# The copy of the low value tile on GpSimd, behind the masks and the weighting, from chunk 2 on

## The chip, the core and the metric

The kernel runs on one core of a Trainium2 chip. The metric is the time of one execution in microseconds (us) on the device. The core has five engines with queues of their own, each executed in order: TensorE (PE in the profile, PEld for its weight loads), VectorE (DVE), ScalarE (ACT), GpSimd (POOL) and SyncE (SP). They wait for each other through semaphores.

## The reference

Two layers follow each other. The first is causal attention with a forget gate, over 8 batches, 8 heads, 576 positions and 64 values a head; the second is a dense layer with a GELU between two products, over 4608 tokens.

```python
# q, k, v: (8, 8, 576, 64), f: (8, 8, 576)
scores = scale * np.matmul(q, k.transpose(0, 1, 3, 2))
cum = np.cumsum(np.log(np.clip(f, 0.0001, 1.0)), axis=-1)
scores = np.where(causal, -1000000000.0, scores + cum[:, :, :, None] - cum[:, :, None, :])
attn = softmax(scores)                                  # with its maximum subtracted
x = matmul(attn, v).transpose(0, 2, 1, 3).reshape(4608, 512)
h = x @ w_in                                            # w_in: (512, 2048)
out = gelu_tanh(h) @ w_out                              # w_out: (2048, 512)
```

## The kernel before

**Attention.** The 64 pairs of batch and head are worked as 16 quads of four heads, quad i from 0 to 15. The decay is folded into the values: `make_vw` multiplies the values of a quad by a weight for each key (line 214) and writes the bf16 tile `vw[i % 2]`, of which there are two. The mul is made by GpSimd where the order says `VW` and by VectorE where it says `vw`. The tile has five slots for the 576 keys in blocks of 128, and a sixth, `LOW`. From quad 2 on, the first 64 queries with the first 64 keys are a piece of their own, whose keys lie on partitions 64 to 127; `copy_low` (line 219) therefore copies the values of those 64 keys from slot 0, partitions 0 to 63, into slot `LOW`, partitions 64 to 127. That is 64 partitions by 256 bf16 values. It can be made once `make_vw` of the same quad is done, and the product that reads it is the next one of that quad.

The other steps of a quad are, by their words in the order: `TK` and `TQ`, transposes of keys and queries by VectorE (line 197); `S`, a third of the scores on TensorE (line 260), with the exponential by ScalarE (line 268); `M`, causal masks by GpSimd with affine selects (line 274), or `m`, the same by a product on VectorE (line 303); `D`, the denominators: a product with the weights themselves (tile `w_bf`, line 328), then transpose, reciprocal and transpose on VectorE (lines 347 to 351); `V`, the two halves of attention times values (tiles `vw` and `po`, line 328), each followed by a VectorE mul into `xT` (line 359). The accumulator `po` has one buffer, so the second `V` waits until VectorE has read the first.

**Dense layers.** The tokens are worked in nine chunks c of 512. The products of chunk c are cut into seven instead of eight (sums of blocks made beforehand), with `P` and `R` for the first layer (lines 373 and 432) and `F`, `f` and `O` for so many matmuls of the second (line 527). VectorE adds the partial products of the second layer from PSUM (line 552, tiles `o_st` and `snap`); TensorE's next product into the same bank waits for that. `T` are the sums of blocks for the next chunk (line 405). `LK`, `LQ` load keys and queries through GpSimd's DMA queue (line 191).

**Order.** The order is written out by hand, as words in `FRONT` and, for chunks 2 to 8, in `TABLES`; every engine's queue holds its instructions in that order. `q3` in the table of chunk c stands for quad 2c + 3, so chunk 2 starts on quads 7 (`q3`) and 8 (`q4`). `CL` is the copy of the low tile. Before the change the words about it in chunks 3 to 5 are

```
VW.q3 f.18 S.q3.2 V.q2.1 M.q3.2 TK.q5 CL.q3 f.16 S.q4.0 VW.q4 D.q3
M.q4.0 f.18 S.q4.1 TQ.q5 V.q3.0 M.q4.1 f.13 V.q3.1 T f.3 CL.q4 S.q4.2
```

Chunk 2 has the same words there. Chunk 6 has only quad 15 left, so one `CL`. On VectorE `CL.q3` thus stands behind the transposes of keys `TK.q5` and ahead of an add of line 552, `D.q3`, a second add, `TQ.q5` and the mul of `V.q3.0`. On GpSimd `VW.q3` stands ahead of the masks `M.q3.2`, which stand ahead of `VW.q4`.

Of the kernel before, what the change touches and what calls it, by code (L numbers as in the profile page):

```python
# [16 lines left out]
def kernel(  # L17
# [10 lines left out]
    nc = tc.nc  # L28

    B, H, S, D = q.shape  # L30
# [36 lines left out]
    LOW, HIGH = NT, NT - 1  # L67
# [18 lines left out]
    TABLES = {}  # L86
    TABLES[2] = """
        Y O.512 P.0.1 R.1 P.4.1 R.1 R.1 TK.q3 TQ.q3 LK.q5 LQ.q5 m.q2.1 M.q2.2.2 m.q2.0 m.q2.2.3 CL.q2 LV P.2 G.0 P.3 K.3.0 K.3.1 K.3.2 P.6 P.7 K.3.3
        G.1.1.2 X F.10 S.q3.0 D.q2 M.q3.0 f.22 S.q3.1 V.q2.0 TK.q4 TQ.q4 M.q3.1 VW.q3 f.18 S.q3.2 V.q2.1 M.q3.2 TK.q5 CL.q3 f.16 S.q4.0 VW.q4 D.q3
        M.q4.0 f.18 S.q4.1 TQ.q5 V.q3.0 M.q4.1 f.13 V.q3.1 T f.3 CL.q4 S.q4.2  # L90
    """
    TABLES[3] = """
        Y O.512 LK.q4 LQ.q4 P.0.1 R.1 P.4.1 R.1 R.1 LK.q5 LQ.q5 M.q2.2 LV R.3 P.2.1 R.3 G.0.1.2 P.6 R.3 G.0.3.4 G.1.1.2 X F.10 S.q3.0 D.q2 M.q3.0
        f.22 S.q3.1 V.q2.0 TK.q4 TQ.q4 M.q3.1 VW.q3 f.18 S.q3.2 V.q2.1 M.q3.2 TK.q5 CL.q3 f.16 S.q4.0 VW.q4 D.q3 M.q4.0 f.18 S.q4.1 TQ.q5 V.q3.0
        M.q4.1 f.13 V.q3.1 T f.3 CL.q4 S.q4.2
    """
    TABLES[4] = """
        Y O.512 LK.q4 LQ.q4 P.0.1 R.1 P.4.1 R.1 R.1 LK.q5 LQ.q5 M.q2.2 LV R.3 P.2.1 R.3 G.0.1.2 P.6 R.3 G.0.3.4 G.1.1.2 X F.10 S.q3.0 D.q2 M.q3.0
        f.22 S.q3.1 V.q2.0 TK.q4 TQ.q4 M.q3.1 VW.q3 f.18 S.q3.2 V.q2.1 M.q3.2 TK.q5 CL.q3 f.16 S.q4.0 VW.q4 D.q3 M.q4.0 f.18 S.q4.1 TQ.q5 V.q3.0
        M.q4.1 f.13 V.q3.1 T f.3 CL.q4 S.q4.2  # L100
    """
    TABLES[5] = """
        Y O.512 LK.q4 LQ.q4 P.0.1 R.1 P.4.1 R.1 R.1 LK.q5 LQ.q5 M.q2.2 LV R.3 P.2.1 R.3 G.0.1.2 P.6 R.3 G.0.3.4 G.1.1.2 X F.10 S.q3.0 D.q2 M.q3.0
        f.22 S.q3.1 V.q2.0 TK.q4 TQ.q4 M.q3.1 VW.q3 f.18 S.q3.2 V.q2.1 M.q3.2 TK.q5 CL.q3 f.16 S.q4.0 VW.q4 D.q3 M.q4.0 f.18 S.q4.1 TQ.q5 V.q3.0
        M.q4.1 f.13 V.q3.1 T f.3 CL.q4 S.q4.2
    """
    TABLES[6] = """
        Y O.512 P.0.1 R.1 P.4.1 R.1 R.1 LK.q5 LQ.q5 M.q2.2 LV R.3 P.2.1 R.3 G.0.1.2 P.6 R.3 G.0.3.4 K.0.0 K.0.1 K.0.2 G.1.1.2 X F.10 S.q3.0 D.q2
        M.q3.0 f.22 S.q3.1 V.q2.0 M.q3.1 VW.q3 f.18 S.q3.2 V.q2.1 M.q3.2 CL.q3 f.20 D.q3 f.18 V.q3.0 v.q3.1 T f.14 K.0.3
    """  # L110
    TABLES[7] = """
        Y O.512 R.1.1 R.1 p.2 R.1 R.1 R.0.1 R.1 R.0 p.2 R.0 R.0 R.3.1 R.0 R.3 p.6 R.3 R.3 p.6 R.3 G.0.1.2 G.1.1.2 G.0.3.4 F.40 T
# [14 lines left out]
    def many(n, shape, dtype, name):  # L127
        return [singles.tile(shape, dtype, name=f"{name}{i}") for i in range(n)]
# [10 lines left out]
    vw = many(2, [128, NT + 1, 4, D], BF16, "vw")  # L139
# [5 lines left out]
    u1, u2, u4 = many(3, [128, HF, HD], BF16, "usum")  # L145
# [18 lines left out]
    def load_v(b, h0=0, nh=H, ts=range(NT), eng=nc.sync):  # L164
        ins = []
        for t in ts:
            n = min(128, S - 128 * t)
            ins.append(eng.dma_start(  # L168
                out=v_nat[b % 2][:n, t, h0:h0 + nh, :],
                in_=v[b, h0:h0 + nh, 128 * t:128 * t + n, :].rearrange("h p d -> p h d"),  # L170
            ))
        return ins
# [37 lines left out]
    def make_vw(i, eng, part=None):  # L210
        h0 = 4 * (i % QPB)
        vb = v_nat[(i // QPB) % 2]
        t0, t1 = {None: (0, NT), 0: (0, QA // 128), 1: (QA // 128, NT)}[part]
        eng.tensor_mul(  # L214
            vw[i % 2][:, t0:t1], vb[:, t0:t1, h0:h0 + 4, :],
            wT[:, i, t0:t1, :].unsqueeze(3).to_broadcast([128, t1 - t0, 4, D]))

    def copy_low(i):
        nc.vector.tensor_copy(vw[i % 2][64:128, LOW], vw[i % 2][0:64, 0])

    def key_columns(i, key, h, c):

# [172 lines left out]
    def x_blocks(c):  # L395

        new, old = xT[:, :, CH * c:CH * (c + 1)], xT[:, :, CH * (c - 1):CH * c]
        return [z[:, 2 * a:2 * a + 2, HC * b:HC * (b + 1)] for z in (new, old) for a in range(2) for b in range(2)]
# [8 lines left out]
    def w_blocks(k):  # L407

        n = 256
        a11, a12, a21, a22 = (w_in_sb[:, 2 * b:2 * b + 2, HU * a + n * k:HU * a + n * (k + 1)]  # L410
                              for a in range(2) for b in range(2))
        old = xT[:, :, CH * HOMES[k]:CH * (HOMES[k] + 1)]
        return a11, a12, a21, a22, old[:, 0:2, 0:n], old[:, 0:2, n:], old[:, 2:4, 0:n]
# [8 lines left out]
    def seven_in(c, k, act=0):  # L422

        a11, a12, s3, a22, s1, s2, s4 = w_blocks(k)
        b11, b12, b21, b22, t1, t2, t3, t4 = x_blocks(c)
        pa, pb = (psS.tile([128, 2, 512], FP32, name="ps_ab", tag="s")[:, 0].rearrange("p (j n) -> p j n", j=2) for _ in range(2))
        pc, pd = (psM.tile([128, 2, HC], FP32, name="ps_cd", tag="m") for _ in range(2))

        def multiply(ps, w, x, first):
            for j in range(2):  # L430
                for dt in range(2):
                    nc.tensor.matmul(ps[:, j], w[:, dt, 128 * j:128 * j + 128], x[:, dt],  # L432
                                     start=(first and j == 0 and dt == 0), stop=(dt == 1),
                                     skip_group_check=True)

        def part():
            return snap_pool.tile([128, 2, HC], FP32, name="snap", tag="snap")

        def gelu(i, j, x):
            ft = N_FT // 2 * i + 2 * k  # L440
            nc.scalar.activation(gT[:, ft:ft + 2, HC * j:HC * (j + 1)], x, AF.Gelu_apprx_tanh)  # L441

        multiply(pa, a11, b11, True)
        p1, u2, v4 = part(), part(), part()
        if act:
            nc.scalar.copy(p1, pa)
            yield
        else:
            nc.vector.tensor_copy(p1, pa)
        multiply(pb, s2, t2, True)  # L450
        nc.vector.tensor_add(u2, pb, p1)
        multiply(pc, s1, t1, True)
        nc.vector.tensor_add(v4, pc, u2)
        multiply(pd, s3, t3, True)
        nc.vector.tensor_add(v4, pd, v4)  # L455
        multiply(pa, a12, b21, False)
        gelu(0, 0, pa)
        yield
        gelu(1, 1, v4)
        multiply(pc, s4, b22, False)  # L460
        nc.vector.tensor_add(p1, pc, u2)
        if not act:
            gelu(0, 1, p1)
        yield
        multiply(pd, a22, t4, False)
        nc.vector.tensor_add(u2, pd, u2)
        if act:
            yield
            gelu(0, 1, p1)
        gelu(1, 0, u2)  # L470
        yield

# [169 lines left out]
    def triangles(copy):  # L642
        for m in causal:
            copy(m, utri_f32)
        copy(causal[1][64:128, 0:64], utri_f32[0:64, 0:64])

    def sums_before(eng):
        eng.tensor_copy(before[:, 0:BH], logfT[:, 0:BH])
        for t in range(1, NT - 1):
            eng.tensor_add(before[:, t * BH:(t + 1) * BH],  # L650
                                 before[:, (t - 1) * BH:t * BH],
                                 logfT[:, t * BH:(t + 1) * BH])
# [25 lines left out]
    def cast_w(copy):  # L678
        copy(w_bf[:, :, 0:NT, :], wT)
        copy(w_bf[64:128, :, LOW, :], wT[0:64, :, 0, :])  # L680

    def load_values(b, half):
        return load_v(b, 4 * half, 4)

    ops = {
        "W": lambda: cast_w(nc.vector.tensor_copy),
        "w": lambda: cast_w(nc.scalar.copy),
        "CW": make_w,
        "SB": lambda: sums_before(nc.gpsimd),
        "sb": lambda: sums_before(nc.vector),  # L690
        "Z": zeros,
        "TR": lambda: triangles(nc.vector.tensor_copy),
        "tr": lambda: triangles(nc.scalar.copy),
# [6 lines left out]
        "v": lambda i, x, *part: attn_out(i, x, True, *part),  # L700
        "VW": lambda i, *part: make_vw(i, nc.gpsimd, *part),
        "vw": lambda i, *part: make_vw(i, nc.vector, *part),
        "CL": copy_low,
        "TK": transpose_k,
        "TQ": transpose_q,
        "LK": lambda i: load_one(k, k_c, i),
# [33 lines left out]
    def quads(call):  # L740
        return lambda c, i, *more: call(i, *more) if i < NQ else None
# [6 lines left out]
        "f": lambda c, n: out_part(c, n, 1),  # L748
        "P": lambda c, pr, spare=0: mlp_in(c, (pr,), spare),
        "R": lambda c, k, *how: next(units.setdefault((c, k), seven_in(c, k, *how))),  # L750
        "p": lambda c, pr: next(halves.setdefault((c, pr), mlp_in_halves(c, pr))),
        "TT": lambda c, *which: x_sums(c, which or range(4), nc.vector),
# [4 lines left out]
        "K": lambda c, k, *which: w_sums(k, nc.vector, which),  # L757
        "k": lambda c, k, *which: w_sums(k, nc.gpsimd, which),
        "LV": lambda c: load_v(c + 2) if c + 2 < B else None,
        **{name: quads(ops[name]) for name in "S M m D V v VW vw CL TK TQ LK LQ".split()},  # L760
    }

    def play(c):
# [40 lines left out]
```

## Time and profile before

| | |
|---|---|
| median of 3 runs | 326.45 us (326.24 to 327.14) |
| profiled execution, its own time | 326.83 us |
| span of its instructions | 325.1 us |
| busy: PE, DVE, ACT, POOL | 312.4, 255.9, 206.8, 107.3 us |
| copies of the low tile (line 219), all on DVE | 14, together 5.7 us |
| granted TensorE clock | 0.999 |

The span runs from the first to the last instruction of the profiled execution; its own time is 1.7 us longer. PE is busy for 96% of the span. A busy time says nothing on whether the end hangs on it: that is read from the waits.

### The profile page before, as it was taken

To read this page: it belongs to the slowest core of one execution; us is meant where nothing else is said; L and a number is where in the kernel's file an instruction comes from. 1 tells how busy PE (TensorE), PEld (TensorE's weight loads), DVE (VectorE), ACT (ScalarE), POOL (GpSimd) and SP (SyncE) were. 2 spreads that over 40 slices of the span, in tenths; PEclk is the share of its full clock that TensorE was granted. 3 is DMA by queue.
4 is the path that set the end of the run, shared out by engine and by line. 5 is a ranking of instruction groups with operands and counts; after the bars stand their busy time and mean duration, and the time that the engine had idled before them with its cause. 6 is when DMAs were issued, how large, how long until landed. Compare 5 with 4: busy or idle time off the path is not lost.

```text
span 325.1 us, 12342 instructions
## 1 busy us (share of the span) xinstructions
PE 312.4 (96%) x5527; PEld 219.0 (67%) x5547; DVE 255.9 (79%) x407; ACT 206.8 (64%) x259; POOL 107.3 (33%) x150
## 2 busy tenths in 40 slices
PE   3999999999999999899999999999999999999995
PEld 1357844544867567576777677667766788788784
DVE  5576138896779899968996899789977979896882
ACT  4685676775857686477857785678666843732830
POOL 8986563440320218410563047302720150000000
PEclk9999999999999999999999999999999999999999
DMA  7999999879102931393119711891120012003013
GB/s 134 202 210 214 181 228 190 163 154 228 49 4 86 176 58 36 67 241 86 36 49 175 172 36 37 150 209 37 34 69 0 4 36 100 2 32 100 0 34 97
DMA packets 46485, 33.45 MB, mean 103 GB/s; under 512 B 29792, under 2 KB 40160, under 8 KB 46432
## 3 DMA queue, kind: packets, MB, share of 16 engines
q0 software_dynamic: 8624, 15.99, 28.3%
q1 hardware_dynamic: 37664, 16.60, 19.4%
q8 instruction: 43, 0.70, 0.9%
q14 instruction: 10, 0.08, 0.1%
q10 hardware_dynamic: 144, 0.07, 0.1%
HBM read 36.85 MB, written 9.44 MB: 142 GB/s over the span
## 4 chain that ended last, share of the span: by engine, by line
PE 87%; DVE 7%; POOL 2%; issue 2%; ACT 1%; POOLq 0%; DVEq 0%; ACTq 0%
PE ps_w L527 27%; PE ps_h L373 14%; PE ps_s L260 9%; PE po L328 9%; PE ps_cd L432 8%; PE ps_ab L432 6%; PE ps_h L481 4%; PE pso L597 4%; PE ps_h L387 2%; PE po_m L314 1%; PE idle_ps L239 1%; DVE pt L303 1%; ACT pt L268 1%; POOL v_nat L168 1%; DVE kT L197 1%
## 5 line engine op out<-in xcount | busy, mean ns | idle before, releaser
L268 ACT ACTIVATE pt<-ps_s 128x1024 bf16<-128x1024 f32 (+2 forms) x100 | 93.7, 988 | 38.5 <-PE ps_s L260 33.1
L274 POOL TENSOR_SCALAR_AFFINE_SELECT pt<-pt 128x512 bf16<-128x512 bf16 (+3 forms) x65 | 38.7, 604 | 115.2 <-ACT pt L268 114.2
L373 PE MATMUL ps_h<-xT,w_in_sb 128*128 128x512 bf16 x228 | 54.5, 379 | 0.6
L527 PEld LDWEIGHTS <-gT 128*32 128x32 bf16 (+1 forms) x1247 | 50.6, 97 | 6.0 <-issue 1.7
L527 PE MATMUL ps_w<-w_out_sb,gT 128*32 128x256 bf16 (+1 forms) x1050 | 46.9, 273 | 0.0
L380 ACT ACTIVATE gT<-ps_h 128x1024 bf16<-128x1024 f32 x30 | 30.6, 1020 | 17.2 <-PE ps_h L373 16.7
L527 PEld LDWEIGHTS <-gsum 128*32 128x32 bf16 (+1 forms) x1256 | 39.2, 97 | 2.5 <-issue 1.1
L373 PEld LDWEIGHTS <-w_in_sb 128*128 128x128 bf16 x240 | 23.4, 98 | 24.3 <-issue 0.4
L260 PE MATMUL ps_s<-qT,kT 32*128 32x64 bf16 (+5 forms) x896 | 36.4, 264 | 0.1
L197 DVE STREAM_TRANSPOSE kT<-k_c 128x576 f32<-128x576 f32 x16 | 19.9, 1245 | 14.1 <-DMA k_c<-in_k_dram 14.1
L527 PE MATMUL ps_w<-usum,gsum 128*32 128x256 bf16 (+1 forms) x832 | 30.6, 273 | 0.0
L214 POOL TENSOR_TENSOR vw<-v_nat,wT 128x1280 bf16<-128x1280 f32 (+1 forms) x13 | 30.3, 2333 | 0.1
L260 PEld LDWEIGHTS <-kT 32*128 32x128 bf16 x896 | 16.5, 93 | 17.1 <-issue 12.0
L441 ACT ACTIVATE gT<-snap 128x512 bf16<-128x512 f32 x45 | 26.1, 625 | 3.0 <-DVE snap L455 2.4
L432 PEld LDWEIGHTS <-w_in_sb 128*128 128x128 bf16 x240 | 23.4, 98 | 6.2 <-issue 1.5
L552 DVE TENSOR_TENSOR o_st<-ps_w,snap 128x512 f32<-128x512 f32 x31 | 21.3, 687 | 7.5 <-PE ps_w L527 6.1
L328 PE MATMUL po<-pt,vw 128*32 128x64 bf16 (+4 forms) x624 | 22.5, 278 | 0.7 <-DVE xT L359 0.7
L359 DVE TENSOR_TENSOR xT<-po,rb 128x576 bf16<-128x576 f32 x26 | 19.5, 751 | 3.8 <-PE po L328 3.3
L328 PEld LDWEIGHTS <-vw 128*32 128x32 bf16 x672 | 14.3, 97 | 11.3 <-issue 4.6
L432 PEld LDWEIGHTS <-xT 128*128 128x128 bf16 x180 | 17.6, 98 | 5.2
L197 DVE STREAM_TRANSPOSE qT<-q_c 128x576 f32<-128x576 f32 x16 | 19.9, 1245 | 0.9 <-PE ps_s L260 0.7
L191 POOL DMA_DIRECT2D k_c<-in_k_dram x16 | 9.2, 576 | 27.8 <-DVE kT L197 22.4
(104 smaller groups left out, 478.1 us busy)
## 6 DMA issues: line engine op xcount, KB each, us to landing
out_dram<-o_st SPq DMA_DIRECT2D x35, 256.0 KB, 2.2
k_c<-in_k_dram POOLq DMA_DIRECT2D x16, 288.0 KB, 5.5
q_c<-in_q_dram POOLq DMA_DIRECT2D x16, 288.0 KB, 7.2
v_nat<-in_v_dram SPq DMA_DIRECT2D x16, 256.0 KB, 6.1
v_nat<-in_v_dram SPq DMA_DIRECT2D x20, 128.0 KB, 4.7
w_in_sb<-in_moe_w_in_dram POOLq DMA_DIRECT2D x4, 512.0 KB, 10.0
w_out_sb<-in_moe_w_out_dram POOLq DMA_DIRECT2D x4, 512.0 KB, 8.6
v_nat<-in_v_dram POOLq DMA_DIRECT2D x9, 128.0 KB, 7.1
```

Of the source, the lines that this page charges most:

```text
L197: nc.vector.transpose(out=dst.rearrange("p s c -> p (s c)").bitcast(FP32) .rearrange("p (t a) -> p a t", a=S // 32), in_=src.rearrange("p ...
L214: eng.tensor_mul(vw[i % 2][:, t0:t1], vb[:, t0:t1, h0:h0 + 4, :], wT[:, i, t0:t1, :].unsqueeze(3).to_broadcast([128, t1 - t0, 4, D]))
L260: nc.tensor.matmul(tiles[h // 2][:, h % 2, c0:c0 + nq], key_columns(i, key, h, c), qq[32 * h:32 * h + 32, q0:q0 + nq, c], start=(c == 0 an ...
L268: nc.scalar.activation(p[:, 2 * g:2 * g + 2, off:off + n], t[:, :, 0:n], AF.Exp, scale=scale)
L274: nc.gpsimd.affine_select(out=x, in_=x, compare_op=ALU.is_ge, fill=0.0, base=0, pattern=pattern, channel_multiplier=-1)
L328: nc.tensor.matmul(po[r0:r0 + w.shape[-1], 448 + q0:448 + q0 + nq], w, p[:, h, col:col + nq], start=(key in (0, "low")), stop=(key in ("lo ...
L373: nc.tensor.matmul(ph[:, j, :], w_in_sb[:, dt, 128 * ft:128 * ft + 128], xT[:, dt, CH * c:CH * (c + 1)], start=(dt == 0), stop=(dt == N_DT ...
L380: nc.scalar.activation(gT[:, 2 * pr:2 * pr + 2, :], ph, AF.Gelu_apprx_tanh)
L432: nc.tensor.matmul(ps[:, j], w[:, dt, 128 * j:128 * j + 128], x[:, dt], start=(first and j == 0 and dt == 0), stop=(dt == 1), skip_group_c ...
L441: nc.scalar.activation(gT[:, ft:ft + 2, HC * j:HC * (j + 1)], x, AF.Gelu_apprx_tanh)
L527: nc.tensor.matmul(ps[c0:c0 + width, n, cols[0]:cols[1]], x[:, j, 128 * n + c0:128 * n + c0 + width], w[:, j, cols[0]:cols[1]], start=(fir ...
L552: nc.vector.tensor_add(st, ps, kept[name])
```

## The change

Nine of the 14 copies are given to GpSimd: `CL.q3` and `CL.q4` of chunks 2 to 5 and `CL.q3` of chunk 6 become `cl.q3` and `cl.q4`. They also change place. `cl.q3` stands ahead of `TK.q5`, which on GpSimd's queue is behind the two masks `M.q3.2` and ahead of `VW.q4`; `cl.q4` stands right behind `VW.q4` and ahead of the masks `M.q4.0`. The copies of quads 2 to 6 (in `FRONT`, and `CL.q2` in chunk 2) stay with VectorE.

```diff
-        ... V.q2.1 M.q3.2 TK.q5 CL.q3 f.16 S.q4.0 VW.q4 D.q3 M.q4.0 f.18 S.q4.1 TQ.q5 V.q3.0
-        M.q4.1 f.13 V.q3.1 T f.3 CL.q4 S.q4.2
+        ... V.q2.1 M.q3.2 cl.q3 TK.q5 f.16 S.q4.0 VW.q4 cl.q4 D.q3 M.q4.0 f.18 S.q4.1 TQ.q5
+        V.q3.0 M.q4.1 f.13 V.q3.1 T f.3 S.q4.2
...
-    def copy_low(i):
-        nc.vector.tensor_copy(vw[i % 2][64:128, LOW], vw[i % 2][0:64, 0])
+    def copy_low(i, eng):
+        eng.tensor_copy(vw[i % 2][64:128, LOW], vw[i % 2][0:64, 0])
...
         multiply(pd, a22, t4, False)
-        nc.vector.tensor_add(u2, pd, u2)
+        if act > 1:
+            z = part()
+            nc.scalar.copy(z, pd)
+            nc.gpsimd.tensor_add(u2, z, u2)
+        else:
+            nc.vector.tensor_add(u2, pd, u2)
...
+        if act > 1:
+            yield
...
-        "CL": copy_low,
+        "CL": lambda i: copy_low(i, nc.vector),
+        "cl": lambda i: copy_low(i, nc.gpsimd),
```

The first two lines stand for the tables of chunks 2 to 5; the table of chunk 6 has `CL.q3` turned into `cl.q3` at its old place. The branches with `act > 1` in `seven_in` are entered by no word: every `R` in the tables gives `act` as 0 or 1.

More of the change, by code (lines that the diff above doesn't have):

```diff
@@ L88 @@
         Y O.512 P.0.1 R.1 P.4.1 R.1 R.1 TK.q3 TQ.q3 LK.q5 LQ.q5 m.q2.1 M.q2.2.2 m.q2.0 m.q2.2.3 CL.q2 LV P.2 G.0 P.3 K.3.0 K.3.1 K.3.2 P.6 P.7 K.3.3
-        G.1.1.2 X F.10 S.q3.0 D.q2 M.q3.0 f.22 S.q3.1 V.q2.0 TK.q4 TQ.q4 M.q3.1 VW.q3 f.18 S.q3.2 V.q2.1 M.q3.2 TK.q5 CL.q3 f.16 S.q4.0 VW.q4 D.q3
-        M.q4.0 f.18 S.q4.1 TQ.q5 V.q3.0 M.q4.1 f.13 V.q3.1 T f.3 CL.q4 S.q4.2
+        G.1.1.2 X F.10 S.q3.0 D.q2 M.q3.0 f.22 S.q3.1 V.q2.0 TK.q4 TQ.q4 M.q3.1 VW.q3 f.18 S.q3.2 V.q2.1 M.q3.2 cl.q3 TK.q5 f.16 S.q4.0 VW.q4 cl.q4
+        D.q3 M.q4.0 f.18 S.q4.1 TQ.q5 V.q3.0 M.q4.1 f.13 V.q3.1 T f.3 S.q4.2
     """
@@ L93 @@
         Y O.512 LK.q4 LQ.q4 P.0.1 R.1 P.4.1 R.1 R.1 LK.q5 LQ.q5 M.q2.2 LV R.3 P.2.1 R.3 G.0.1.2 P.6 R.3 G.0.3.4 G.1.1.2 X F.10 S.q3.0 D.q2 M.q3.0
-        f.22 S.q3.1 V.q2.0 TK.q4 TQ.q4 M.q3.1 VW.q3 f.18 S.q3.2 V.q2.1 M.q3.2 TK.q5 CL.q3 f.16 S.q4.0 VW.q4 D.q3 M.q4.0 f.18 S.q4.1 TQ.q5 V.q3.0
-        M.q4.1 f.13 V.q3.1 T f.3 CL.q4 S.q4.2
+        f.22 S.q3.1 V.q2.0 TK.q4 TQ.q4 M.q3.1 VW.q3 f.18 S.q3.2 V.q2.1 M.q3.2 cl.q3 TK.q5 f.16 S.q4.0 VW.q4 cl.q4 D.q3 M.q4.0 f.18 S.q4.1 TQ.q5
+        V.q3.0 M.q4.1 f.13 V.q3.1 T f.3 S.q4.2
     """
@@ L98 @@
         Y O.512 LK.q4 LQ.q4 P.0.1 R.1 P.4.1 R.1 R.1 LK.q5 LQ.q5 M.q2.2 LV R.3 P.2.1 R.3 G.0.1.2 P.6 R.3 G.0.3.4 G.1.1.2 X F.10 S.q3.0 D.q2 M.q3.0
-        f.22 S.q3.1 V.q2.0 TK.q4 TQ.q4 M.q3.1 VW.q3 f.18 S.q3.2 V.q2.1 M.q3.2 TK.q5 CL.q3 f.16 S.q4.0 VW.q4 D.q3 M.q4.0 f.18 S.q4.1 TQ.q5 V.q3.0
-        M.q4.1 f.13 V.q3.1 T f.3 CL.q4 S.q4.2
+        f.22 S.q3.1 V.q2.0 TK.q4 TQ.q4 M.q3.1 VW.q3 f.18 S.q3.2 V.q2.1 M.q3.2 cl.q3 TK.q5 f.16 S.q4.0 VW.q4 cl.q4 D.q3 M.q4.0 f.18 S.q4.1 TQ.q5
+        V.q3.0 M.q4.1 f.13 V.q3.1 T f.3 S.q4.2
     """
@@ L103 @@
         Y O.512 LK.q4 LQ.q4 P.0.1 R.1 P.4.1 R.1 R.1 LK.q5 LQ.q5 M.q2.2 LV R.3 P.2.1 R.3 G.0.1.2 P.6 R.3 G.0.3.4 G.1.1.2 X F.10 S.q3.0 D.q2 M.q3.0
-        f.22 S.q3.1 V.q2.0 TK.q4 TQ.q4 M.q3.1 VW.q3 f.18 S.q3.2 V.q2.1 M.q3.2 TK.q5 CL.q3 f.16 S.q4.0 VW.q4 D.q3 M.q4.0 f.18 S.q4.1 TQ.q5 V.q3.0
-        M.q4.1 f.13 V.q3.1 T f.3 CL.q4 S.q4.2
+        f.22 S.q3.1 V.q2.0 TK.q4 TQ.q4 M.q3.1 VW.q3 f.18 S.q3.2 V.q2.1 M.q3.2 cl.q3 TK.q5 f.16 S.q4.0 VW.q4 cl.q4 D.q3 M.q4.0 f.18 S.q4.1 TQ.q5
+        V.q3.0 M.q4.1 f.13 V.q3.1 T f.3 S.q4.2
     """
@@ L108 @@
         Y O.512 P.0.1 R.1 P.4.1 R.1 R.1 LK.q5 LQ.q5 M.q2.2 LV R.3 P.2.1 R.3 G.0.1.2 P.6 R.3 G.0.3.4 K.0.0 K.0.1 K.0.2 G.1.1.2 X F.10 S.q3.0 D.q2
-        M.q3.0 f.22 S.q3.1 V.q2.0 M.q3.1 VW.q3 f.18 S.q3.2 V.q2.1 M.q3.2 CL.q3 f.20 D.q3 f.18 V.q3.0 v.q3.1 T f.14 K.0.3
+        M.q3.0 f.22 S.q3.1 V.q2.0 M.q3.1 VW.q3 f.18 S.q3.2 V.q2.1 M.q3.2 cl.q3 f.20 D.q3 f.18 V.q3.0 v.q3.1 T f.14 K.0.3
     """
@@ L759 @@
         "LV": lambda c: load_v(c + 2) if c + 2 < B else None,
-        **{name: quads(ops[name]) for name in "S M m D V v VW vw CL TK TQ LK LQ".split()},
+        **{name: quads(ops[name]) for name in "S M m D V v VW vw CL cl TK TQ LK LQ".split()},
     }
```

## The prediction

> **What bounds the kernel now.** The page comes first, and in it the busy times of the engines.
>
> ```profile
> PE 312.4 (96%) x5527; PEld 219.0 (67%) x5547; DVE 255.9 (79%) x407; ACT 206.8 (64%) x259; POOL 107.3 (33%) x150
> ```
>
> TensorE is the bound: 12.7 us of the span of 325.1 are left. Work taken from VectorE is worth something only where TensorE waits for VectorE, so the second view is the busy time by windows, here chunk 2's end and one whole period of chunk 3 (columns: window, its length, then busy us and instruction count of PE, PEld, DVE, ACT and POOL, clock, DMA share, GB/s).
>
> ```profile
> 126.00:138.00 12.00, 10.34 (x313) 7.60 (x302) 11.43 (x17) 5.45 (x7) 7.50 (x11) 1.00 0.23 44
> 138.00:172.00 34.00, 33.89 (x727) 24.48 (x728) 29.61 (x47) 24.23 (x31) 12.14 (x16) 1.00 0.46 106
> ```
>
> In chunk 3 TensorE idles 0.11 us in 34, and the same windows of chunks 4 and 5 give 0.16 and 0.11. In 126 to 138 it idles 1.66 us in 12. The third view, TensorE's waits (us in total, times, longest), names them; the two fall at 130 and 134 us:
>
> ```profile
> PE ps_w L527 <- DVE o_st L552: 0.9, 1, 0.9
> PE po L328 <- DVE xT L359: 0.7, 1, 0.7
> ```
>
> The other waits of that list over 0.3 us lie before 10 us or are not laid to an engine. The chain of waits says the same: it is on VectorE from 108.2 to 130.8 and almost wholly on TensorE from there to 320.8. The fourth view is the line of the copy itself (ns, min/median/max):
>
> ```profile
> L219 DVE COPY vw<-vw x14: 220/221/2070, 54.7 to 263.3; 64x256 bf16<-64x256 bf16 x14
> ```
>
> One copy took 2070 ns, nine times the median. It is `CL.q3` of chunk 2, and the timelines of POOL and of DVE show what it ran beside (start, us):
>
> ```profile
> 127.64 2.33 POOL L214 TENSOR_TENSOR vw<-v_nat,wT 128x1280 bf16<-128x1280 f32 x1
> ```
> ```profile
> 127.98 2.07 DVE L219 COPY vw<-vw 64x256 bf16<-64x256 bf16 x1
> 130.08 0.69 DVE L552 TENSOR_TENSOR o_st<-ps_w,snap 128x512 f32<-128x512 f32 x1
> ```
>
> GpSimd's weighting `VW.q4` began 0.34 us earlier and ended at 129.97; the copy ended at 130.05. It depends only on `VW.q3`, done at 126.17, so this was no wait on a semaphore: the copy was held until the weighting was over. In chunk 3 the copy came 0.31 us ahead of the weighting and took 0.42:
>
> ```profile
> 163.10 0.42 DVE L219 COPY vw<-vw 64x256 bf16<-64x256 bf16 x1
> ```
> ```profile
> 163.41 2.33 POOL L214 TENSOR_TENSOR vw<-v_nat,wT 128x1280 bf16<-128x1280 f32 x1
> ```
>
> Chunks 4 and 5 are as chunk 3 (0.42 and 0.43). The Trainium skill, "SBUF — State Buffer", section "SBUF: two separate sides", says that VectorE and GpSimd share one pair of ports as an exclusive lock, kept by whoever starts first for a whole instruction; by that rule the trace agrees, with 2.07 us for a copy of 0.22.
>
> What the held copy cost is read from TensorE's timeline, from the denominators (`w_bf`) of quad `q3` to the second `V` of it, first in chunk 2 and then in chunk 3:
>
> ```profile
> 127.49 0.86 PE L328 MATMUL po<-pt,w_bf 128*32 128x512 bf16 x24
> ...
> 130.82 0.62 PE L527 MATMUL ps_w<-w_out_sb,gsum 128*32 128x256 bf16 x16 [0.94 <-DVE o_st L552]
> ...
> 134.95 0.87 PE L328 MATMUL po<-pt,vw 128*32 128x512 bf16 x24 [0.73 <-DVE xT L359]
> ```
> ```profile
> 163.21 0.86 PE L328 MATMUL po<-pt,w_bf 128*32 128x512 bf16 x24
> ...
> 168.65 0.86 PE L328 MATMUL po<-pt,vw 128*32 128x512 bf16 x24
> ```
>
> The same matmuls take 134.95 - 127.49 = 7.46 us in chunk 2 and 168.65 - 163.21 = 5.44 in chunk 3 (chunks 4 and 5: 5.44 as well). The difference is 2.02 us. The two recorded waits sum to 1.67; the other 0.35 is the pipeline that empties and refills twice (a matmul of line 527 lasts 0.27 us in its row, but 56 of them start within 1.53).
>
> **Part 1: the copies taken from VectorE.** Nine go: four `CL.q3` of 2.07, 0.42, 0.42 and 0.43 us in chunks 2 to 5, four `CL.q4` of 0.22, and one of 0.22 in chunk 6; 4.4 us of VectorE. In chunks 3 to 6 TensorE waits nowhere for VectorE, so these are worth nothing. In chunk 2 the add of line 552 follows the transpose, so it starts at 127.98 in place of 130.08, and ends at 128.67. TensorE wants that bank 1.53 us after 128.18, at 129.71: the first wait is gone with 1.0 us to spare. What is late next? From this add to the end of the mul into `xT` VectorE works without a break; in chunk 3 that is 163.54 to 168.36, 4.82 us. In chunk 2 the add now starts 0.49 after the denominators, so the mul ends at 0.49 + 4.82 = 5.31, and TensorE asks for it at 5.44, if it runs as in chunk 3. The second wait goes too, with 0.13 to spare. The gain is 2.02 us if chunk 2 becomes like chunk 3, and 1.67 if only the recorded idle goes. I take 2.02, since three chunks with the same words measure 5.44. The four copies `CL.q4` stood behind the sums `T`; nothing waits for them.
>
> **Part 2: the copies put on GpSimd.** No row shows this copy there. The nearest have the same 64 partitions and 256 bf16 values, or the same operation:
>
> ```profile
> L274 POOL TENSOR_SCALAR_AFFINE_SELECT pt<-pt 64x256 bf16<-64x256 bf16 x12 | 4.9, 410 | 82.8 <-ACT pt L268 82.6
> ...
> L648 POOL COPY gsum<-gsum 128x64 f32<-128x64 f32 x1 | 0.3, 257 | 0.0
> ```
>
> I take 0.41 us, from the select of this very size, with 0.26 below and 2.33 (the weighting, GpSimd's longest row here) above; none of these moves data to other partitions, which is why I keep the upper end. Nine are 3.7 us on an engine that is busy a third of the span.
>
> On GpSimd's queue `cl.q3` waits for `VW.q3`, which was done before the masks ahead of it ended, so for nothing. Behind it stand `VW.q4`, `cl.q4`, which waits for it, the masks `M.q4.0` and the four loads of keys and queries. All move back by two copies, 0.82 us. The last mask of `M.q4.0` waits for ScalarE anyway: GpSimd idles 3.05 us ahead of it in chunk 2 and 1.93 in chunk 3, which covers them. Were that cover gone, the loads would come later, but the keys issued at 134.70 are transposed at 158.99. The product of `q4` is a chunk later.
>
> The only near reader is TensorE: one weight load in the first `V` of quad `q3` now waits for GpSimd, in chunks 2 to 6. In chunk 3 the masks end at 163.43 and those weights are loaded from 166.53, so the copy has 3.1 us (chunks 4 and 5: 3.1; chunk 2, with its first wait gone, 3.1 to 3.2). In chunk 6 the masks end at 264.57 and the loads begin at 266.58: 2.0 us. At 0.41 us nothing waits. At 2.33 it costs 0.3 us, in chunk 6 alone.
>
> **Sum.** Profiled execution: 326.83 - 2.02 = 324.8 us. The median of the runs was 0.38 lower, so 326.45 - 2.02 = 324.4. The bounds: a gain of 1.67 - 0.3 = 1.35 gives 325.1; 2.02 and all the idle of the windows of chunks 3 to 5 (0.38) give 324.05. The branches with `act > 1` are never entered and cost nothing.
>
> **Rivals.** *The conflict turned round.* GpSimd's copy holds up VectorE beside it, 0.41 us each. In chunks 3 to 5 VectorE loses 0.82 and is relieved of 0.44, so the mul into `xT` comes 0.38 later; it has 0.29 less 0.05 for the signal, so TensorE waits 0.14 in each, 0.42 in all. In chunk 2 it has 0.13 - 0.05, so it waits 0.74. The gain shrinks to 2.02 - 1.16 = 0.86: 325.6 us. Against it: beside GpSimd's weightings the transposes and the adds from PSUM take 0.77 and 0.69 us, as elsewhere, and these are what would run beside the new copies; only the bf16 copy was ever held. The Trainium skill, "Perfetto Trace Analysis", section "Optimizing Scalar/DVE Operations", warns that moving work between these two engines might not help because they share a port; here that is this rival. A chance of 0.10.
>
> *Nothing to gain.* The order of copy and weighting in chunk 2 is decided by 0.34 us. If most timed runs fell as chunk 3 does, their 326.45 held no such wait, and the time stays at 326.4. Against it: the profiled execution, with the wait, was within the spread of the three runs and only 0.38 above their median, not 2. Chance 0.10.
>
> *A slow copy.* Moving 64 partitions to 64 others may cost GpSimd more than any row shows. TensorE then waits (x - 3.1) in four chunks and (x - 2.0) in chunk 6 at the load of the low tile. That eats the 2.02 at x = 3.3 us and makes the kernel slower by 1 us at 3.5; at twice the weighting, 4.66, it is 4 x 1.56 + 2.66 = 8.9, less 2.02: 333.3 us. For it is only that no row shows such a move; against it, that 3.5 us is eight times the select of that size. Chance 0.08.
>
> **How the numbers follow.** A measurement of this kernel can tell 0.3%, 1.0 us, from no change. The forecast has 0.72 and lies from 324.0 to 325.1; with the first rival, and a little for the median's own spread below, the range is 323.9 to 325.6, which leaves out the other two. Faster by over 0.3%: 0.72 and some of the first rival, 0.76. Within 0.3%: the rest of it and the second, 0.16. Slower: 0.08.
>
> **What would show it.** Right: five copies of line 219 on DVE with none near 2 us, nine on POOL near 0.4; the add of line 552 in chunk 2 starting right behind the transpose; no wait of TensorE for `o_st` or `xT` in chunk 2, and 5.44 us from its denominators to the second `V`; PE busy still 312. Wrong: weight loads of `vw` waiting for POOL (the third rival), VectorE rows stretched beside the new copies (the first), or another wait of TensorE at the same place.

## The result and the profile after

The changed kernel takes 324.94 us (median of 6 runs, 324.16 to 325.06) against 326.65 us for the kernel before (median of 6, 326.24 to 327.14): a ratio of 0.9944, 95% interval 0.9933 to 0.9954 (a ratio here is not the quotient of the two medians, which is 0.9948). The profiled execution took 325.06 us with a span of 323.3. In the code after, what stands behind the new branch in `seven_in` is seven lines lower: line 527 is now 534, 552 is 559; 219, 328 and 359 are where they were.

First the line of the copy in the trace after (ns, min/median/max). Nine copies are on GpSimd, none on VectorE is long, and all nine take the same 391 ns, so no row among them shows that it was held:

```profile
L219 POOL COPY vw<-vw x9: 391/391/392, 128.0 to 262.8; 64x256 bf16<-64x256 bf16 x9
L219 DVE COPY vw<-vw x5: 221/222/325, 55.0 to 114.0; 64x256 bf16<-64x256 bf16 x5
```

The timeline of GpSimd in chunk 2 shows the new order: masks, copy, weighting, copy.

```profile
126.70 1.22 POOL L274 TENSOR_SCALAR_AFFINE_SELECT pt<-pt 128x512 bf16<-128x512 bf16 x2 [0.27 <-ACT pt L268]
127.99 0.39 POOL L219 COPY vw<-vw 64x256 bf16<-64x256 bf16 x1
128.46 2.33 POOL L214 TENSOR_TENSOR vw<-v_nat,wT 128x1280 bf16<-128x1280 f32 x1
130.86 0.39 POOL L219 COPY vw<-vw 64x256 bf16<-64x256 bf16 x1
```

On VectorE's timeline the add follows the transpose directly. The end of the add and the denominators' transposes run beside the weighting of 128.46 to 130.79, and none of them is stretched (over the whole kernel such adds have a mean of 0.685 us, these transposes of 0.78):

```profile
126.98 1.23 DVE L197 STREAM_TRANSPOSE kT<-k_c 128x576 f32<-128x576 f32 x1
128.06 0.67 DVE L559 TENSOR_TENSOR o_st<-ps_w,snap 128x512 f32<-128x512 f32 x1
128.68 0.78 DVE L347 STREAM_TRANSPOSE den<-po 128x576 f32<-128x576 f32 x1
```

TensorE's timeline has no bracket any more between the denominators and the second `V` of that quad, and 133.19 - 127.75 = 5.44 us between their starts, where there were 7.46:

```profile
127.75 0.86 PE L328 MATMUL po<-pt,w_bf 128*32 128x512 bf16 x24
...
129.97 0.61 PE L534 MATMUL ps_w<-w_out_sb,gsum 128*32 128x256 bf16 x16
...
133.19 0.86 PE L328 MATMUL po<-pt,vw 128*32 128x512 bf16 x24
```

The windows (PE busy first) say the same: 0.05 us of idle in the 12 us that held 1.66, and 0.10 in the 34 us behind them, where there was 0.11.

```profile
126.00:138.00 12.00, 11.95 (x328) 8.65 (x322) 10.44 (x17) 7.47 (x8) 9.59 (x15) 1.00 0.36 76
138.00:172.00 34.00, 33.90 (x729) 24.61 (x730) 28.56 (x43) 24.21 (x32) 13.67 (x19) 1.00 0.48 103
```

PE's busy time is 312.4 us as before, and VectorE's share of the chain of waits has gone from 7% to 1%.

### The profile page after: what moved, and what is told of

Read it like the earlier page. It is cut to its first block, busy times and chain, and to the rows that moved or that the text cites. A ratio compares the mean times of both kernels' runs of the same rounds, so it can differ in the third digit from the quotient of the medians.

```text
span 323.3 us, 12343 instructions
## 1 busy us (share of the span) xinstructions
PE 312.4 (97%) x5527; PEld 219.3 (68%) x5547; DVE 250.8 (78%) x398; ACT 206.8 (64%) x259; POOL 110.9 (34%) x159
## 4 chain that ended last, share of the span: by engine, by line
PE 93%; ACT 2%; POOL 2%; issue 1%; DVE 1%; POOLq 0%; DVEq 0%; ACTq 0%
PE ps_w L534 30%; PE ps_h L373 16%; PE po L328 10%; PE ps_s L260 9%; PE ps_cd L432 8%; PE ps_ab L432 6%; PE ps_h L488 4%; PE pso L604 4%; ACT pt L268 2%; PE ps_h L387 2%; PE po_m L314 1%; PE idle_ps L239 1%; POOL v_nat L168 1%; PE ps_o L328 0%; DVE pt L303 0%
```

## The experiments

The theory: the whole gain is one copy, `CL.q3` of chunk 2, which VectorE could not run while GpSimd's weighting ran. The rivals: that any work taken from VectorE counts, or that GpSimd's queue and its slack decide. In each run the number that tells is the time from the start of the denominators of `q3` to the start of its second `V` ("the stretch"; 7.46 us in chunk 2 before, 5.44 after). All ratios are against the kernel before, which was timed again beside the experiments: its median was 326.66 us for the first four and 326.86 us for the last three.

**Only that one copy.** The diff against the kernel before, in the table of chunk 2 alone:

```diff
- V.q2.1 M.q3.2 TK.q5 CL.q3 f.16 S.q4.0 VW.q4 D.q3
+ V.q2.1 M.q3.2 cl.q3 TK.q5 f.16 S.q4.0 VW.q4 D.q3
```

> Only the copy CL.q3 of chunk 2 goes to GpSimd, ahead of TK.q5; the other eight stay on VectorE as before. Theory (the held copy): the whole gain is the one copy of 2.07 us, so 324.9 us, and 5.44 us from the denominators to the second V of chunk 2. Rival (less work on VectorE): that copy is 0.22 us of work like the others, so a ninth of the 1.7 us, 326.45 us, or at most what its share of busy time is worth.

Measured: 325.23 us (ratio 0.9954, interval 0.9941 to 0.9967), the stretch in chunk 2 133.12 - 127.69 = 5.43 us. This one copy brings the gain: the interval overlaps that of the full change, and the ninth that "less work" gives, 0.9994, lies outside it. The time is 0.3 us above the expected 324.9, but none of that lies with the eight copies left on VectorE: from the denominators of chunk 2 to the first product of line 432 in chunk 7, behind the last copy, TensorE takes 268.93 - 127.69 = 141.24 us here and 269.01 - 127.75 = 141.26 in the full change. That holds although one of the eight was held as well, by a mask that began 0.01 us ahead of it in chunk 6 (DVE and POOL; the first of the two masks ends at 262.04, the copy at 262.13):

```profile
261.42 0.71 DVE L219 COPY vw<-vw 64x256 bf16<-64x256 bf16 x1 [0.43 <-POOL vw L214]
```
```profile
261.41 1.22 POOL L274 TENSOR_SCALAR_AFFINE_SELECT pt<-pt 128x512 bf16<-128x512 bf16 x2
```

TensorE waited for nothing there.

**All but that one.** Against the changed kernel, in chunk 2:

```diff
- V.q2.1 M.q3.2 cl.q3 TK.q5 f.16 S.q4.0 VW.q4 cl.q4
+ V.q2.1 M.q3.2 TK.q5 CL.q3 f.16 S.q4.0 VW.q4 cl.q4
```

> Eight copies go to GpSimd and only CL.q3 of chunk 2 stays on VectorE, at its old place behind TK.q5. Theory (the held copy): that copy is held by the weighting again, about 2 us in its row and 7.46 us from the denominators to the second V; no gain, 326.6 us. Rival (less work on VectorE): eight ninths of the 1.7 us, 325.1 us.

Measured: 326.78 us (1.0004, 0.9995 to 1.0013), the stretch 134.89 - 127.43 = 7.46 us. The waits of TensorE are back, and the copy again ends with the weighting, at 129.99 against 129.91 (DVE and POOL timelines of this kernel):

```profile
127.92 2.07 DVE L219 COPY vw<-vw 64x256 bf16<-64x256 bf16 x1
```
```profile
127.58 2.33 POOL L214 TENSOR_TENSOR vw<-v_nat,wT 128x1280 bf16<-128x1280 f32 x1
```

Eight copies, 2.4 us of VectorE's work by the rows before (4.4 less 2.07), are worth nothing that these times can tell: the interval leaves them 0.2 us at most.

**The same copy on VectorE, later.** Against the kernel before, in chunk 2 alone; nothing changes engine:

```diff
- TK.q5 CL.q3 f.16 S.q4.0 VW.q4 D.q3 M.q4.0 f.18
+ TK.q5 f.16 S.q4.0 VW.q4 D.q3 CL.q3 M.q4.0 f.18
```

> All copies stay on VectorE; only CL.q3 of chunk 2 stands behind D.q3, so that it starts after GpSimd's weighting has ended. Theory (the held copy): the copy takes 0.22 us, or up to 0.45 beside a mask; the mul into xT, which has 0.13 us to spare, comes up to 0.45 later, so 5.44 to 5.8 us from the denominators to the second V, and 324.9 to 325.3 us. Rival (less work on VectorE): no work has left it, 326.65 us. Rival (it is GpSimd's order that matters): no change of GpSimd's queue, 326.65 us.

Measured: 324.69 us (0.9943, 0.9931 to 0.9956), the stretch 132.42 - 126.82 = 5.60 us. VectorE's timeline (the code stands a line higher in this kernel):

```profile
128.87 0.78 DVE L350 STREAM_TRANSPOSE rb<-rec 128x576 f32<-128x576 f32 x1
129.68 0.22 DVE L218 COPY vw<-vw 64x256 bf16<-64x256 bf16 x1
129.93 0.69 DVE L551 TENSOR_TENSOR o_st<-ps_w,o_st 128x512 f32<-128x512 f32 x1
```

The copy is back at 0.22 us once it stands behind the weighting (126.98 to 129.31 here). The stretch lies in the range expected, the time 0.2 us below it. The gain thus needs neither GpSimd nor less work on VectorE, only that the two operations do not meet. The copy still puts the mul into `xT` back: it starts 131.63 - 126.82 = 4.81 us behind the denominators in place of 132.15 - 127.75 = 4.40. Of these 0.41 us, 0.16 show in the stretch.

**The collision made three times.** Against the changed kernel, in chunks 3 to 5:

```diff
- V.q2.1 M.q3.2 cl.q3 TK.q5 f.16 S.q4.0 VW.q4 cl.q4 D.q3
+ V.q2.1 M.q3.2 TK.q5 f.16 S.q4.0 VW.q4 CL.q3 cl.q4 D.q3
```

> The changed kernel, but CL.q3 of chunks 3 to 5 stays on VectorE and stands behind VW.q4 in the order, so that VectorE comes to it (behind its add, 0.1 us or so) after the weighting has begun. Theory (the held copy): three rows of 2.0 to 2.3 us; the mul into xT of chunks 3 to 5 ends 1.66 us later, which TensorE feels by 1.4 us in each, 6.9 us from the denominators to the second V: 329.2 us. If the copy still comes first, 0.2 to 0.4 us and 324.9. Rival (work on VectorE): three copies of 0.22 us more, 324.9 to 325.5 us.

Measured: 329.21 us (1.0081, 1.0067 to 1.0095), the stretch 6.92 us in each of the three chunks and 5.44 in chunk 2. Timelines of DVE, POOL and PE in chunk 3:

```profile
161.56 2.21 DVE L219 COPY vw<-vw 64x256 bf16<-64x256 bf16 x1
163.80 0.78 DVE L347 STREAM_TRANSPOSE den<-po 128x576 f32<-128x576 f32 x1
```
```profile
161.36 2.32 POOL L214 TENSOR_TENSOR vw<-v_nat,wT 128x1280 bf16<-128x1280 f32 x1
```
```profile
168.07 0.87 PE L328 MATMUL po<-pt,vw 128*32 128x512 bf16 x24 [1.15 <-DVE xT L359]
```

The weighting was 0.20 us ahead, and the copy waited for the end of it. Three times 6.92 - 5.44 = 1.48 is 4.4 us, and 324.94 + 4.4 = 329.4. The collision was made to order, in chunks whose stretch had been 5.44.

**An operation with two inputs in place of the copy.** Against the kernel before, chunk 2's copy alone:

```diff
-        nc.vector.tensor_copy(vw[i % 2][64:128, LOW], vw[i % 2][0:64, 0])
+        x = vw[i % 2][0:64, 0]
+        nc.vector.tensor_tensor(out=vw[i % 2][64:128, LOW], in0=x, in1=x, op=ALU.max)
```

> The kernel before, with CL.q3 of chunk 2 made by VectorE at its old place as the maximum of the tile with itself: one operation with two inputs from SBUF in place of a copy, about 0.3 us of work by the rows of other bf16 operations of two inputs. Theory (the held copy, a lock on shared ports): an operation with two SBUF inputs is held too, if the lock covers it: a row of about 2.1 us and 326.65 us. Rival (only the fast bf16 copy is held): a row of 0.3 us, no wait of TensorE, 324.9 to 325.1 us.

Measured: 326.56 us (1.0003, 0.9983 to 1.0022), the stretch 134.69 - 127.16 = 7.53 us, and a row of 2.15 us (DVE), again to the end of the weighting (POOL):

```profile
127.64 2.15 DVE L223 TENSOR_TENSOR vw<-vw 64x256 bf16<-64x256 bf16 x1
```
```profile
127.31 2.33 POOL L214 TENSOR_TENSOR vw<-v_nat,wT 128x1280 bf16<-128x1280 f32 x1
```

So it is not the copy as such. The Trainium skill, "SBUF — State Buffer", section "SBUF: two separate sides", counts among the operations that take the shared ports those of VectorE in a mode that uses two ports, and those with two inputs from SBUF, the latter only against a GpSimd operation that reads SBUF, which the weighting does; this run agrees, with 2.15 us. How long this operation takes alone, no run shows. The transposes and the adds with one input from PSUM, 0.78 and 0.67 us beside a weighting in the profile after, were not held.

The kernel before has such a meeting of its own, which the prediction passed over. Near 86 us two VectorE operations with two inputs from SBUF, on other tiles, meet the masks and then a weighting (DVE and POOL):

```profile
86.35 0.93 DVE L510 TENSOR_TENSOR gT<-gT 128x1024 bf16<-128x1024 bf16 x1
87.20 1.14 DVE L512 TENSOR_TENSOR gsum<-gT,gsum 128x1024 bf16<-128x1024 bf16 x1
```
```profile
87.88 2.65 POOL L214 TENSOR_TENSOR vw<-v_nat,wT 128x1280 bf16<-128x1280 f32 x1
```

Their medians over the kernel are 0.68 us each, and the weighting elsewhere takes 2.33: here both engines are held in turn, and no tile is common to the two.

**GpSimd's copy made longer.** In chunks 2 to 5 of the changed kernel `cl.q3` is written ten or five times over:

```diff
- M.q3.2 cl.q3 TK.q5
+ M.q3.2 cl.q3 cl.q3 ... cl.q3 TK.q5
```

> The changed kernel with cl.q3 made ten times over by GpSimd in chunks 2 to 5 (the same data again), each 0.39 us and 0.08 of waiting: 4.7 us in place of 0.4. Theory (3.1 us of slack at the load of the low tile): the first V of q3 waits 1.4 to 1.5 us in each of four chunks, 5.8 us in all: 330.7 us. Rival (GpSimd's queue is the tighter: VW.q4, the masks and the loads behind it, 4.3 us later, cost more): over 332 us, with waits in the chunk behind. Rival (GpSimd has slack to spare): 324.9 us.

> The same with five times, 2.3 us: the last copy of chunk 3 ends near 164.0 in the time of the changed kernel, where the low tile is loaded at 164.9. Theory (3.1 us of slack): free, 324.9 us. Rival (GpSimd's queue is the tighter): 1.9 us later in its queue, 326 us or more.

Measured: ten copies 330.07 us (1.0102, 1.0087 to 1.0117), five 324.93 us (0.9946, 0.9933 to 0.9958), with a stretch of 5.43 us in chunk 2 and 5.44 in chunks 3 to 5, so five are free. With ten, the wait is where the prediction put it, at the load of the low tile, which follows four matmuls on slot 0 (PE and POOL in chunk 3):

```profile
165.73 0.40 PE L328 MATMUL po<-pt,vw 128*32 128x512 bf16 x4
167.25 0.65 PE L328 MATMUL po<-pt,vw 128*32 128x64 bf16 x20 [1.12 <-POOL vw L219]
```
```profile
162.69 4.50 POOL L219 COPY vw<-vw 64x256 bf16<-64x256 bf16 x10
167.28 2.33 POOL L214 TENSOR_TENSOR vw<-v_nat,wT 128x1280 bf16<-128x1280 f32 x1
```

The stretch is 6.69 us in chunk 2 and 6.74 or 6.75 in chunks 3 to 5: 1.25 + 3 x 1.30 = 5.2 us, and 324.94 + 5.2 = 330.1. Of 4.50 us of copies 1.3 were felt, so 3.2 were free. The expectation had 4.7 us of copies and came out 0.6 high. TensorE has no wait for what stands behind them in GpSimd's queue.

## Why the prediction was right

**The held copy.** It was read from two rows that end within 0.1 us of each other. It is no wait on a semaphore: in chunk 6 of the kernel before the copy does wait for its own weighting, and the profile puts those 0.43 us ahead of its row, which is 0.22 us long. The 0.42 us of the copies in chunks 3 to 5, which the prediction left unexplained, fits the same reading: in chunk 3 the copy began during the masks ahead of the weighting, which ended at 163.43, and ended at 163.52. The first four runs show it from both sides: that copy alone gives the gain, the other eight give nothing, the same copy in another place on VectorE gives it too, and three collisions cost 1.48 us each.

**What replaced the two waits.** The first was to go with 1.0 us to spare, the second with 0.13. After, the add ends at 128.73 and the bank is asked for at 129.97, 1.24 us; the mul into `xT` runs from 132.15 to 132.90 and the second `V` starts at 133.19, 0.29. Both margins were underrated by about 0.2: the add was put where the copy had started, 1.27 us behind the start of the transpose, but it starts after 1.08. The margin that was left is what hid 0.25 of the 0.41 us of the third run.

**GpSimd's side.** 0.41 us was taken from the select of that size; the copy measures 0.391, move to other partitions included; no run makes it without the move. The upper bound, 2.33 us as GpSimd's longest row, was misread: a weighting takes up to 2.65. The 3.1 us of slack stand at 3.2. In GpSimd's queue the two copies cost 1.1 us and not 0.82: in chunk 2, from the end of the masks `M.q3.2` to the end of the next masks, it took 131.06 - 127.66 = 3.40 us before and 132.43 - 127.92 = 4.51 after, since gaps of about 0.07 us stand beside each copy. This delay was covered as said: GpSimd's idle ahead of the last mask fell from 1.93 to 0.82 us in chunk 3, and in chunk 2, where that mask itself comes earlier, from 3.05 to 0.83; it still waits for ScalarE.

**The sum.** The term of 2.02 us is confirmed where it was made: the stretch went from 7.46 to 5.44. From the start of those denominators to the end, the span before has 325.1 - 127.49 = 197.6 us and the one after 323.3 - 127.75 = 195.6. By the medians the timed gain is 1.71, and the forecast of 324.4 was 0.5 low. 0.2 of this is the median before, 326.65 over six runs in place of 326.45 over three. The other 0.3 is within what the times can tell: the interval of the ratio is a gain of 1.5 to 2.2 us. In the two profiles it lies far ahead of the change: a product of line 260 that starts at 54.53 us before starts at 54.80 after. From that product to the denominators of chunk 2 all nine profiles take 72.95 to 73.00 us, although these denominators start anywhere between 126.82 and 127.75. So the first 55 us differ from profile to profile, over 70 us ahead of the first instruction that any of these versions changes; what makes them differ, these runs don't show.

**The rivals.** The conflict turned round didn't occur: nine copies of 391 to 392 ns, and VectorE's rows beside them as elsewhere. But the argument against it, that only the bf16 copy was ever held, was wrong, as the rows near 86 us show. The new copies met no operation of a kind that these traces show held, so where VectorE has one beside them, the rival is untested. That there was nothing to gain is refuted by the timed runs, and the slow copy by its row.

No version here beats the changed kernel clearly: the copy later on VectorE measures 0.9943 against 0.9944, and the intervals overlap.

## What to carry to other kernels

Look at the maximum beside the median of a line: one row of nine times the median, ending with a row of another engine, is the sign of a collision. Moving one of the two in the order tests it, and its price is found at the engine that bounds the kernel, by setting the stretch beside the same stretch of a chunk without it. A bf16 copy within SBUF (0.22 us that became 2.07) or an operation with two SBUF inputs (2.15) on VectorE should not be due just after a long GpSimd operation begins. Here moving it in the order cured this as well as moving it to the other engine. The count of moved operations and their busy time says little: eight of the nine were worth nothing, and five times the copy on GpSimd cost nothing.

## What the hardware showed that was not expected

- The copy on VectorE that stood behind the weighting was expected to wait up to 0.45 us for a mask; it took 0.22. It came as the first of two selects had just ended (129.67 on GpSimd, the copy from 129.68 to 129.90), which is a chance of timing: in chunk 6 of the first run a select did hold the copy, for 0.71 us.
- An operation with two inputs, 64 partitions by 256 bf16, was held like the copy: 2.15 us. The prediction left such operations out, though the trace before shows two of them held near 86 us.
- The hold goes both ways. In chunk 6 of the kernel before, the copy and a select start at 263.26 together; the copy takes its 0.22 us, and the select 0.72 in place of 0.64.
- Copies that follow each other on GpSimd start 0.46 us apart ((4.50 - 0.39) / 9 for ten), 0.07 more than the row of one.
